# The load of the next batch's z one column later, and the Strassen form for three more tiles, in an attention unit followed by an MoE layer

## The chip, the cores and the metric

The kernel runs on one core of a Trainium2 chip. The metric is the device time of one execution in microseconds (us). In ten executions the kernel before took 1233.96 us in the median (1233.74 to 1235.21).

## The reference

```python
batch, seq, d_model = (8, 3008, 256); d_qk = 64
scores = scale * np.matmul(z, z.transpose(0, 2, 1))     # scale = 1 / seq
attn = np.maximum(scores, 0.0) ** 2
x = (u * np.matmul(attn, v)).reshape(batch * seq, d_model)
h = x @ w_in                                            # d_ff = 2048
g = h * np.cos(h)
out = (g @ w_out).astype(np.float32)
```

All inputs and the output are float32; the kernel computes on float16 tiles and sums in float32.

## The kernel before, in words

**Tiles and stages.** The 3008 rows of a batch are six columns J of 512 (the last one 448). Eight batches make NSLOT = 48 stages s = 6 b + J. A stage has two phases on TensorE. In *phase A* (`phase_a`) the attention output of column s is summed over all rows (L258), into the two PSUM banks M for the first half of d and a pair of banks E for the second. Between these matmuls stand the score matmuls (L191) of later columns, about 3 stages ahead, each followed by relu on ScalarE (L204) and square on VectorE (L209, L212). The scores are symmetric, so half of them are not computed but transposed by a DMA that SP (SyncE) issues (L238, L244). At its end `gate_sum` (L269, L270) and `gate_mul` (L286) make x = u * attention; the second half of the product is made by GpSimd (POOL) at the beginning of phase B.

In *phase B* (`phase_b`) the MoE layer runs on 512 rows, called tile m. It holds h of tile s-1 and y of tile s-2. h comes in eight *units* of two 128-wide blocks of d_ff: four matmuls into one tile E (L403), cos by ScalarE into c (L411), and g = h * cos on VectorE (L414). There are three tiles E, so a unit's matmuls wait for the g of the third unit before. The units come in the order 0, 4, 1, 5, 2, 6, 3, 7. Tile g has two buffers (`gpool`): g of tile m takes the buffer of tile m-2. Tile x has two buffers as well.

**The Strassen form.** For tiles that `mixed` names (2 to 45, without those of 384 rows: 5, 17, 29, 41) y is not four plain products over 256 rows, but the seven of a Strassen scheme (the Winograd variant), each 16 matmuls of 128 x 128 (L465): 112 matmuls of 128 columns instead of 64 of 256. They need sums of blocks of g: `mix_early` on GpSimd makes s1 and a difference in place (L427, L428) once g is there, four pairs a tile; `mix_late` on VectorE makes s2 and s4 (L433, L435) during phase A of the next stage. The products run in the order 5, 1, 6, 7, 2, 3, 4 (`order_y`), one after each h unit, in turns into the banks M[0] and M[1]; the results are scaled and added by ScalarE (L484), VectorE (L478) and GpSimd (L487, L490), and SP stores them (L529). The other tiles are plain: `emit_y` has two blocks of d_ff for all rows (L507), `store_y` copies (L537) and stores. The last tile has a function of its own, `last_y`, which computes y row block by row block and stores each at once.

**The order.** The order of each engine's instructions is the order of the calls, written by hand (`manual_schedule`); waits between engines follow from the tiles that they share. All loads of u, v and z are issued by GpSimd and convert to float16 (L118, L124, L140, L146), each tile as a whole in its turn of GpSimd's queue. All DMA transpositions are issued by SP.

**z.** The z of batch b+1 goes through one buffer (`zpool`) in two halves. `load_z` loads a half twice, side by side (L118; the second half has four small issues L124 as well), `turn_z` transposes it by DMA into zT (L133). In the main loop, for b > 0: `load_z(b+1, 0)` behind phase A of J=0; `turn_z(b+1, 0)` and straight behind it `load_z(b+1, 1)` behind phase A of J=1; `turn_z(b+1, 1)` behind phase A of J=2. The second load overwrites the buffer that the first transposition reads. For b = 0 the same pair stands behind phase B of stage 2.

**The start.** Stages 0 to 2 have phases A of their own (`phase_a_first`). Four units of tile 0 stand between those of stages 1 and 2; phase B of stage 2 has units 4 to 7 of tile 0 and 0 to 5 of tile 1, that of stage 3 the last two of tile 1 and then all of tile 2. The end: phase B of stage 46 has h of tile 45 and y of 44, stage 47 h of 46 and y of 45, stage 48 (no phase A) h of 47 and y of 46; then `last_y(47)`.

Of the kernel before, what the change touches and what calls it, by code (L numbers as in the profile page):

```python
# [10 lines left out]
FP32 = mybir.dt.float32  # L11
# [3 lines left out]
def kernel(  # L15
# [9 lines left out]
    nc = tc.nc  # L25
# [77 lines left out]
    def take_e():  # L103
        i = e_order.pop(0)
        e_order.append(i)
        return i
# [119 lines left out]
    def emit_turns(due, more=0):  # L226
        while turns and (turns[0][0] <= due or more > 0):
            if turns[0][0] > due:
                more -= 1
            (b, c), key = turns.pop(0)  # L230
            b, J, I = key
            i = turn_slots[key]
            a = piece_bufs[i]
            if I == J:
                a4 = a.rearrange("p (k w) -> p k w", w=CW)
                for rr in range(2, 4):
                    rows = P if J * 4 + rr < NB - 1 else H
                    nc.sync.dma_start_transpose(  # L238
                        a4[:, 0:2, rr * P:rr * P + rows],
                        a[0:rows, rr * CW:rr * CW + 2 * P],  # L240
                    )
            else:
                d = new_piece((b, I, J))
                nc.sync.dma_start_transpose(d.rearrange("p (n j) -> p n j", j=P), a)  # L244
            if pending.pop(i) == "dropped":
                free_pieces.append(i)
# [146 lines left out]
    def mwidth(m):  # L393
        return 3 * P if m % (2 * NC) == NC - 1 else CW
# [21 lines left out]
        )  # L416

    def mixed(m):
        return 2 <= m < NSLOT - 2 and mwidth(m) == CW

    F = NFT // 2
    T = 2 * P
# [1 line left out]
    def mix_early(m, j):  # L424
        g, f = gs[m], slice(2 * j, 2 * j + 2)
        lower = slice(F + 2 * j, F + 2 * j + 2)
        nc.gpsimd.tensor_tensor(s1[:, f, :], g[:, f, T:], g[:, lower, T:], ALU.add)  # L427
        nc.gpsimd.tensor_tensor(g[:, f, T:], g[:, f, 0:T], g[:, f, T:], ALU.subtract)  # L428
# [18 lines left out]

    order_y = (5, 1, 6, 7, 2, 3, 4)

    def product(m, n):  # L450
        g = gs[m]
        t = lambda i: w_mix[:, i, :, :]
        left, right = {
            1: (g[:, 0:F, 0:T], w_out16[:, 0:F, 0:P]),
            2: (g[:, F:, 0:T], w_out16[:, F:, 0:P]),
            3: (s4, w_out16[:, F:, P:D]),
            4: (g[:, F:, T:], t(3)),
            5: (s1, t(0)),
            6: (s2, t(1)),
            7: (g[:, 0:F, T:], t(2)),  # L460
        }[n]
        acc = M[order_y.index(n) % 2][:, 0:T]
        for ft in range(F):
            for k in range(2):
                nc.tensor.matmul(  # L465
                    acc[:, k * P:(k + 1) * P],
                    left[:, ft, k * P:(k + 1) * P],
                    right[:, ft, :],
                    start=(ft == 0 and k == 0),
                    stop=(ft == F - 1 and k == 1),  # L470
                )
        acc = acc.rearrange("p (k d) -> p k d", d=P)
        if n == 5:
            y_outs[m] = [opool.tile([P, 2, D], FP32, name="o") for i in range(2)]
            y_parts[m] = {}
        c11, c12, c21, c22 = (y_outs[m][i][:, :, d * P:(d + 1) * P] for i in range(2) for d in range(2))
        parts = y_parts[m]
        add = lambda dst, other: nc.vector.scalar_tensor_tensor(  # L478
            dst, acc, inv_s2, other, ALU.mult, ALU.add
        )  # L480
        if n in (1, 5, 6):
            parts[n] = ypool.tile([P, 2, P], FP32, name=f"p{n}")
        if n in (1, 5):
            nc.scalar.activation(parts[n], acc, AF.Copy, bias=0.0, scale=inv_s2)  # L484
        elif n == 6:
            add(parts[6], parts[1])
            nc.gpsimd.tensor_tensor(c12, parts[6], parts[5], ALU.add)  # L487
        elif n == 7:
            add(c21, parts[6])
            nc.gpsimd.tensor_tensor(c22, c21, parts[5], ALU.add)  # L490
        elif n == 2:
            add(c11, parts[1])
        elif n == 3:
            add(c12, c12)
            store_half(m, 0, y_outs[m][0])
        else:
            add(c21, c21)
            store_half(m, 1, y_outs[m][1])

    def y_bank(m, k):  # L500
        if m == NSLOT - 1 and k == 3:
            return E[0][:, 0, 0:D]
        return M[k // 2][:, (k % 2) * D:(k % 2 + 1) * D]

    def y_block(m, ft, k):
        final = m == NSLOT - 1
        nc.tensor.matmul(  # L507
            y_bank(m, k),
            gs[m][:, ft, k * P:(k + 1) * P],
            w_out16[:, ft, :],  # L510
            start=(ft == 0 and (k % 2 == 0 or (final and k == 3))),
            stop=(ft == NFT - 1 and (k % 2 == 1 or k == mwidth(m) // P - 1 or (final and k == 2))),
        )

    def emit_y(m, i):
# [17 lines left out]
    def store_y(m):  # L533
        for half in range(2):
            n = min(2, mwidth(m) // P - 2 * half)
            o = opool.tile([P, 2, D], FP32, name="o")
            nc.scalar.activation(  # L537
                o[:, 0:n, :],
                M[half].rearrange("p (k d) -> p k d", d=D)[:, 0:n, :],
                AF.Copy, bias=0.0, scale=inv_s2,  # L540
            )
            store_half(m, half, o)

    def last_y(m):
        b, J = m // NC, m % NC
        for ft in range(NFT):
            y_block(m, ft, 0)
            y_block(m, ft, 1)
        for k in range(4):
            if k >= 2:  # L550
                for ft in range(NFT):
                    y_block(m, ft, k)
            o = opool.tile([P, 2, D], FP32, name="o")
            nc.scalar.activation(
                o[:, 0, :], y_bank(m, k),
                AF.Copy, bias=0.0, scale=inv_s2,
            )
            t0 = b * S + J * CW + k * P
            if k < 3:
                nc.sync.dma_start(out[t0:t0 + P, :], o[:, 0, :])  # L560
            else:
                nc.sync.dma_start(out[t0:t0 + H, :], o[0:H, 0, :])
                nc.scalar.dma_start(out[b * S - H:b * S, :], o[H:P, 0, :])

    def phase_b(s):
        y, hs = s - 2, [(s - 1, i) for i in (0, 4, 1, 5, 2, 6, 3, 7)]
        if s == 2:
            hs = [(0, i) for i in range(4, 8)] + [(1, i) for i in range(6)]
        elif s == 3:
            hs = [(1, 6), (1, 7)] + hs  # L570
        elif s == NSLOT + 1:
            hs = []
        for dh in range(len(late_sums)):
            gate_mul(s, 2 - len(late_sums), late_sums.pop(0), nc.gpsimd)
        if mixed(y):
            ys = [lambda n=n: product(y, n) for n in order_y]
        else:
            ys = [lambda i=i: emit_y(y, i) for i in range(8)]
            if len(hs) == 8:
                six, seven = ys[6:]  # L580
                ys[6:] = [lambda: (six(), seven(), store_y(y))]
            else:
                ys[7] = lambda f=ys[7]: (f(), store_y(y))
        n = 0
        for i, (m, unit) in enumerate(hs):
            times_c = emit_h(m, unit)
            if not mixed(y):
                times_c()
            if i < len(ys):
                ys[i]()  # L590
            if mixed(y):
                times_c()
            if mixed(m) and unit >= 4:
                mix_early(m, unit - 4)
            if i in (1, 3, 5):
                emit_turns((0, 0), 1)

    parts0 = [(4 * g, 4 * g + 4) for g in range(NC)]
    nc.vector.memset(warm, 0.0)
# [82 lines left out]
    phase_a_first(0, 12, {4: lambda: turn_late(4), 8: lambda: turn_late(5)})  # L682
    phase_a_first(1, 12)
    nc.gpsimd.dma_start(w_out16, moe_w_out.rearrange("(k p) f -> p k f", p=P))
    for i in range(4):
        emit_h(0, i)()
    phase_a_first(2, 14)
    assert done_groups[0] == need[3]
# [10 lines left out]
    for s in range(3, NSLOT + 1):  # L699
        b, J = s // NC, s % NC  # L700
        if s < NSLOT - 2:
            load_u(s + 2)
        if s < NSLOT:
            phase_a(s)
        if b + 1 < B:
            if b > 0 and J == 0:
                load_z(b + 1, 0)
            if b > 0 and J == 1:
                turn_z(b + 1, 0)
                load_z(b + 1, 1)  # L710
            if J == (2 if b > 0 else 3):
                turn_z(b + 1, 1)
            if J == NC - 2:
                load_v(b + 1, 0)
            if J == NC - 1:
                for g in range(1, NC):
                    load_v(b + 1, g)
        if s < NSLOT - 2:
            turn_u(s + 2)
        phase_b(s)  # L720
# [31 lines left out]
```

## Time and profile before

| | |
|---|---|
| median of ten executions | 1233.96 us |
| the profiled execution | 1235.2 us |
| its span, first to last instruction | 1233.4 us |
| TensorE matmul busy | 1196.5 us (97%) |
| VectorE, ScalarE, GpSimd busy | 990.9, 796.2, 645.6 us |
| phase B of an undisturbed stage with a full tile in Strassen form | 13.27 us |
| mean granted TensorE clock | 0.989 |

In the lines of the profile PE is TensorE (PEld its weight loads), DVE VectorE, ACT ScalarE, POOL GpSimd, SP SyncE, with a q where the queue alone issues. L118 is line 118 of the kernel, `out<-in` the tiles it writes and reads. A line of the view of waits has who waited at which line, for whom, the sum in us, how often, and the longest. A row of the timeline has start and length in us, engine, line, operation and tiles, how many were merged, and in brackets how long the engine had stood idle before it and what ended that. A row of the groups has, behind the count, busy us and the mean of one in ns, then the idle time before.

### The profile page before, as it was taken

Reading aid. Unit: us, or ns where it says so; the run is one execution under the profiler, and the core shown is the slowest. Engines: PE = TensorE matmul, PEld = TensorE weight load, DVE = VectorE, ACT = ScalarE, POOL = GpSimd, SP = SyncE. Lnnn points to the kernel's source line nnn. Section 1 sums busy time; section 2 is a strip of 40 time slices with the busy share of each in tenths; the row PEclk is TensorE's granted clock in tenths of the full one; section 3 lists DMA queues with packets and bytes.
Section 4 is the critical chain, followed back from the end, with each engine's and each line's share of the span. In section 5 each row is a group of like instructions: output and inputs, shape, how many; then the busy total and the mean of one; then the engine's idle time right before and its main releaser. Section 6 shows DMA issues by size and latency. Waiting matters only on the chain.

```text
span 1233.4 us, 28309 instructions
## 1 busy us (share of the span) xinstructions
PE 1196.5 (97%) x11695; PEld 708.1 (57%) x11695; DVE 990.9 (80%) x1248; ACT 796.2 (65%) x923; POOL 645.6 (52%) x657
## 2 busy tenths in 40 slices
PE   8999999999979999999998999999999799999998
PEld 4455655655546655665564655665566465566566
DVE  6857887889868887788986889778888588978765
ACT  7857676667646666667674667666766467666444
POOL 3155725657455671665645657176563665525540
PEclk9999999999989999999998999999999899999999
DMA  9998897769966599755996469973797635974301
GB/s 154 167 168 142 134 139 101 116 116 134 138 97 107 100 137 152 116 94 107 150 154 100 73 116 143 165 105 77 114 172 123 107 69 107 152 140 87 60 18 53
DMA packets 467410, 145.13 MB, mean 118 GB/s; under 512 B 391760, under 2 KB 467024, under 8 KB 467280
## 3 DMA queue, kind: packets, MB, share of 16 engines
q1 hardware_dynamic: 368304, 110.11, 51.1%
q0 software_dynamic: 97440, 32.78, 26.1%
q8 instruction: 91, 1.49, 0.5%
q10 hardware_dynamic: 1536, 0.43, 0.2%
q14 instruction: 39, 0.32, 0.1%
HBM read 66.32 MB, written 24.64 MB: 74 GB/s over the span
## 4 chain that ended last, share of the span: by engine, by line
PE 86%; POOL 5%; DVE 3%; DMA 2%; issue 2%; ACT 2%; SPq 0%; POOLq 0%; DVEq 0%; ACTq 0%
PE E L403 24%; PE M L465 19%; PE M L258 18%; PE E L258 17%; PE E L191 5%; PE M L507 3%; DMA zT<-z 2%; ACT r L204 1%; POOL s L427 1%; POOL g L428 1%; POOL z L124 1%; POOL z L118 1%; DVE A L209 1%; POOL x L286 1%; DVE sm L270 1%
## 5 line engine op out<-in xcount | busy, mean ns | idle before, releaser
L411 ACT ACTIVATE c<-E 128x1024 f16<-128x1024 f32 (+1 forms) x384 | 386.0, 1007 | 230.8 <-PE E L403 229.9
L414 DVE SCALAR_TENSOR_TENSOR g<-E,c 128x1024 f16<-128x1024 f32 (+1 forms) x384 | 458.4, 1197 | 74.7 <-ACT c L411 74.2
L204 ACT ACTIVATE r<-E 128x512 f16<-128x512 f32 (+1 forms) x342 | 327.9, 967 | 142.1 <-PE E L191 137.2
L258 PEld LDWEIGHTS <-v 64*128 64x128 f16 x4512 | 228.8, 95 | 275.5 <-issue 45.2
L403 PE MATMUL E<-x,w_in 128*128 128x512 f16 (+1 forms) x1408 | 355.2, 375 | 7.6 <-DVE sm L270 6.8
L258 PE MATMUL M<-A,v 64*128 64x512 f16 (+1 forms) x2256 | 288.9, 378 | 21.7 <-DVE o L478 21.4
L258 PE MATMUL E<-A,v 64*128 64x512 f16 (+1 forms) x2256 | 278.1, 372 | 0.0
L427 POOL TENSOR_TENSOR s<-g 128x512 f16<-128x512 f16 x160 | 188.5, 1178 | 141.3 <-DVE g L414 104.6
L428 POOL TENSOR_TENSOR g<-g 128x512 f16<-128x512 f16 x160 | 200.8, 1255 | 12.5
L403 PEld LDWEIGHTS <-w_in 128*128 128x128 f16 x1536 | 135.0, 98 | 118.0 <-issue 28.4
L209 DVE TENSOR_TENSOR A<-r 128x1024 f16<-128x1024 f16 x240 | 175.5, 742 | 22.7 <-ACT r L204 22.1
L465 PEld LDWEIGHTS <-g 128*128 128x128 f16 x2560 | 156.4, 98 | 36.0
L286 POOL TENSOR_TENSOR x<-sm,uT 128x512 f16<-128x512 f32 (+1 forms) x43 | 49.0, 1139 | 192.6 <-DVE sm L270 192.3
L465 PEld LDWEIGHTS <-s 128*128 128x128 f16 x1920 | 117.3, 98 | 27.0
L191 PE MATMUL E<-zT 64*128 64x512 f16 (+2 forms) x684 | 126.8, 363 | 2.2 <-DVE zT L631 1.1
L433 DVE TENSOR_TENSOR s<-s,g 128x1024 f16<-128x1024 f16 x80 | 88.0, 1101 | 13.9 <-POOL s L427 13.9
L118 POOL DMA_DIRECT2D z<-in_z_dram x28 | 29.9, 1071 | 130.5 <-DMA zT<-z 130.5
L212 DVE TENSOR_TENSOR A<-r 128x512 f16<-128x512 f16 (+1 forms) x102 | 79.1, 776 | 19.1 <-ACT r L204 18.9
L465 PE MATMUL M<-w_mix,g 128*128 128x128 f16 x1280 | 84.5, 219 | 0.0
L465 PE MATMUL M<-w_mix,s 128*128 128x128 f16 x1280 | 84.5, 219 | 0.0
L465 PE MATMUL M<-w_out,g 128*128 128x128 f16 x1280 | 84.5, 219 | 0.0
L478 DVE SCALAR_TENSOR_TENSOR o<-M,o 128x256 f32<-128x256 f32 x80 | 34.0, 424 | 41.8 <-POOL o L487 24.0
(55 smaller groups left out, 715.7 us busy)
## 6 DMA issues: line engine op xcount, KB each, us to landing
out_dram<-o SPq DMA_DIRECT2D x87, 256.0 KB, 2.2
v<-in_v_dram POOLq DMA_DIRECT2D x40, 256.0 KB, 8.9
u<-in_u_dram POOLq DMA_DIRECT2D x40, 256.0 KB, 5.0
A<-A SPq DMA_TRANSPOSE x207, 5.1
z<-in_z_dram POOLq DMA_DIRECT2D x14, 192.0 KB, 10.9
z<-in_z_dram POOLq DMA_DIRECT2D x14, 176.0 KB, 4.1
v<-in_v_dram POOLq DMA_DIRECT2D x8, 192.0 KB, 11.9
u<-in_u_dram POOLq DMA_DIRECT2D x8, 192.0 KB, 4.1
```

Source lines behind the costliest of these rows:

```text
L191: nc.tensor.matmul(e[:, t, 0:W], zT[t * H:(t + 1) * H, k * P:(k + 1) * P], zT[t * H:(t + 1) * H, J * CW:J * CW + W], start=True, stop=True,)
L204: nc.scalar.activation(r[:, :, 0:W], e[:, :, 0:W], AF.Relu)
L209: nc.vector.tensor_tensor(a4, r4, r4, ALU.mult)
L212: nc.vector.tensor_tensor(a4, r[:, :, 0:W], r[:, :, 0:W], ALU.mult)
L258: nc.tensor.matmul(bank[:, 0:width(J)], vs[b, k // 4][t * H:(t + 1) * H, k % 4, dh * P:(dh + 1) * P], value_rhs(b, J, k, t), start=start, ...
L403: nc.tensor.matmul(e[:, f, 0:W], w_in16[:, k, ft * P:(ft + 1) * P], x[:, k, 0:W], start=(k == 0), stop=(k == 1),)
L411: nc.scalar.activation(c[:, :, 0:W], e[:, :, 0:W], AF.Sin, bias=half_pi, scale=inv_s2)
L414: return lambda: nc.vector.scalar_tensor_tensor(gs[m][:, 2 * i:2 * i + 2, 0:W], e[:, :, 0:W], 1.0, c[:, :, 0:W], ALU.mult, ALU.mult)
L427: nc.gpsimd.tensor_tensor(s1[:, f, :], g[:, f, T:], g[:, lower, T:], ALU.add)
L428: nc.gpsimd.tensor_tensor(g[:, f, T:], g[:, f, 0:T], g[:, f, T:], ALU.subtract)
L433: nc.vector.tensor_tensor(s2[:, f, :], s1[:, f, :], g[:, f, 0:T], ALU.subtract)
L465: nc.tensor.matmul(acc[:, k * P:(k + 1) * P], left[:, ft, k * P:(k + 1) * P], right[:, ft, :], start=(ft == 0 and k == 0), stop=(ft == F - ...
```

## The change

Three things change.

1. `load_z(b+1, 1)` stands at the beginning of stage J=2 (for b > 0), behind the load of u and ahead of phase A, and no longer directly behind `turn_z(b+1, 0)` in J=1. For b = 0 nothing moves.
2. `mixed` names tiles 1, 46 and 47 too. Two units of tile 0, not four, stand ahead of phase A of stage 2; phase B of stage 2 has 14 units, the last six of tile 0 and all eight of tile 1, and y of tile 0 between them; stage 3 has the eight of tile 2 and the seven products of tile 1.
3. At the end, phase B of stage 46 has four units (0, 4, 1, 5) of tile 46 behind the eight of tile 45; stage 47 the other four of 46 and four of 47; stage 48 the last four of 47. What is summed early for tile 46 is still on GpSimd, in stage 47; for tile 47 it is on VectorE (`last_early`). The late sums of 46 and 47 (`mix_late`) stand between the g of these phases. `last_y` has seven products in the order 1, 2, 4, 5, 7, 6, 3, in the banks M and in two tiles E of two banks each.

`multiply`, `add_to` and `copy_to` are `product` cut into parts, for `last_y`.

```diff
     def mixed(m):
-        return 2 <= m < NSLOT - 2 and mwidth(m) == CW
+        return 1 <= m and mwidth(m) == CW
...
+    def last_early(m, c):
+        g, f = gs[m], slice(4 * c, 4 * c + 4)
+        lower = slice(F + 4 * c, F + 4 * c + 4)
+        nc.vector.tensor_tensor(s1[:, f, :], g[:, f, T:], g[:, lower, T:], ALU.add)
+        nc.vector.tensor_tensor(g[:, f, T:], g[:, f, 0:T], g[:, f, T:], ALU.subtract)
+
     def last_y(m):
         b, J = m // NC, m % NC
-        for ft in range(NFT):
-            y_block(m, ft, 0)
-            y_block(m, ft, 1)
-        for k in range(4):
...
+        t0 = b * S + J * CW
+        ea, eb = E[take_e()], E[take_e()]
+        banks = {1: M[1], 2: M[0], 4: ea[:, 0, :], 5: ea[:, 1, :], 7: eb[:, 0, :], 6: eb[:, 1, :], 3: M[1]}
+        o = [opool.tile([P, 2, D], FP32, name="o") for i in range(2)]
...
+        for n in (1, 2, 4, 5, 7, 6, 3):
+            multiply(m, n, banks[n][:, 0:T])
+            acc = banks[n][:, 0:T].rearrange("p (k d) -> p k d", d=P)
+            if n == 1:
+                copy_to(p[1], acc)
+            elif n == 2:
+                add_to(c11, acc, p[1])
+                nc.sync.dma_start(
+                    out[t0:t0 + T, 0:P].rearrange("(k p) d -> p k d", p=P), c11
+                )
+            elif n == 4:
+                copy_to(c21, acc)
+            elif n == 5:
+                copy_to(p[5], acc)
+                nc.gpsimd.tensor_tensor(c12, p[1], p[5], ALU.add)
+            elif n == 7:
+                add_to(c22, acc, p[1])
+            elif n == 6:
+                add_to(c12, acc, c12)
+                add_to(p[6], acc, c22)
+                nc.vector.tensor_tensor(c22, p[6], p[5], ALU.add)
+                nc.vector.tensor_tensor(c21, p[6], c21, ALU.add)
+                store_half(m, 1, o[1])
             else:
...
+                for k, eng in enumerate((nc.sync, nc.scalar)):
+                    add_to(c12[:, k, :], acc[:, k, :], c12[:, k, :])
+                    eng.dma_start(out[t0 + k * P:t0 + (k + 1) * P, P:D], c12[:, k, :])
 
     def phase_b(s):
         y, hs = s - 2, [(s - 1, i) for i in (0, 4, 1, 5, 2, 6, 3, 7)]
         if s == 2:
-            hs = [(0, i) for i in range(4, 8)] + [(1, i) for i in range(6)]
-        elif s == 3:
-            hs = [(1, 6), (1, 7)] + hs
-        elif s == NSLOT + 1:
-            hs = []
+            hs = [(0, i) for i in range(2, 8)] + hs
+        elif s == NSLOT - 2:
+            hs = hs + [(s, i) for i in (0, 4, 1, 5)]
+        elif s == NSLOT - 1:
+            hs = hs[4:] + [(s, i) for i in (0, 4, 1, 5)]
+        elif s == NSLOT:
+            hs = hs[4:]
...
+        tail = {}
+        if s == NSLOT - 1:
+            tail = {
+                1: [lambda: [mix_early(s - 1, j) for j in range(3)]],
+                3: [lambda: mix_early(s - 1, 3)],
+                4: [lambda: mix_late(s - 1, "s2", 0)],
+                5: [lambda: mix_late(s - 1, "s2", 1)],
+                6: [lambda: mix_late(s - 1, "s4", 0)],
+                7: [lambda: mix_late(s - 1, "s4", 1)],
+            }
+        if s == NSLOT:
+            after = (0, 1, 2)
+        elif s == NSLOT - 2:
+            after = (0, 2, 3, 5, 7, 8, 10)
+        elif n > 8:
+            after = (1, 2, 4, 5, 7, 8, 10, 11)
+        elif mixed(y):
+            after = range(7)
+        else:
+            after = (0, 1, 2, 3, 4, 5, 6, 6)
...
-            if i < len(ys):
-                ys[i]()
+            for f, place in zip(ys, after):
+                if place == i:
+                    f()
             if mixed(y):
                 times_c()
-            if mixed(m) and unit >= 4:
+            if mixed(m) and unit >= 4 and m < NSLOT - 2:
                 mix_early(m, unit - 4)
+            for f in tail.get(i, ()):
+                f()
+            if s == NSLOT and i in (1, 3):
+                last_early(s - 1, i // 2)
             if i in (1, 3, 5):
                 emit_turns((0, 0), 1)
+        if s == NSLOT:
+            ys[3]()
+            ys[4]()
+            mix_late(s - 1, "s2", 0)
+            ys[5]()
+            mix_late(s - 1, "s2", 1)
+            ys[6]()
+            mix_late(s - 1, "s4", 0)
+            mix_late(s - 1, "s4", 1)
...
-    for i in range(4):
+    for i in range(2):
         emit_h(0, i)()
     phase_a_first(2, 14)
...
         if s < NSLOT - 2:
             load_u(s + 2)
+        if b > 0 and J == 2 and b + 1 < B:
+            load_z(b + 1, 1)
         if s < NSLOT:
             phase_a(s)
...
             if b > 0 and J == 1:
                 turn_z(b + 1, 0)
-                load_z(b + 1, 1)
```

In `phase_b`, `after` says behind which unit each part of y stands; `ys` are these parts.

## The prediction

> **What bounds the kernel now.** I read the page's shares first, then who waited for whom, then the timeline at the waits.
>
> ```profile
> span 1233.4 us, 28309 instructions
> PE 1196.5 (97%) x11695; PEld 708.1 (57%) x11695; DVE 990.9 (80%) x1248; ACT 796.2 (65%) x923; POOL 645.6 (52%) x657
> ```
>
> TensorE is the bound: 36.9 us of the span are not its own. Who owns them, from the view of waits (total, times, longest):
>
> ```profile
> POOL z L118 <- DMA zT<-z: 130.5, 7, 23.3
> ...
> DVE o L478 <- POOL o L487: 24.0, 3, 8.6
> ...
> PE M L258 <- DVE o L478: 21.4, 3, 7.7
> ...
> PE E L403 <- DVE sm L270: 6.8, 4, 2.0
> ```
>
> The first line is GpSimd standing at the load of the second half of the next z. The next two are three times each, so one chain. The timeline of stage 13 (b=2, J=1) shows it:
>
> ```profile
> 336.17 1.04 PE L403 MATMUL E<-x,w_in 128*128 128x512 f16 x4
> ...
> 341.37 1.57 SPq L133 DMA_TRANSPOSE zT<-z  x1
> ...
> 346.66 1.08 POOL L118 DMA_DIRECT2D z<-in_z_dram  x1 [16.29 <-DMA zT<-z]
> ...
> 351.00 1.21 POOL L286 TENSOR_TENSOR x<-sm,uT 128x512 f16<-128x512 f32 x1
> ...
> 354.50 0.72 POOL L487 TENSOR_TENSOR o<-p,p 128x256 f32<-128x256 f32 x1
> ...
> 355.25 0.42 DVE L478 SCALAR_TENSOR_TENSOR o<-M,o 128x256 f32<-128x256 f32 x1 [8.53 <-POOL o L487]
> ...
> 357.19 2.74 PE L258 MATMUL M<-A,v 64*128 64x512 f16 x12 [7.69 <-DVE o L478]
> ```
>
> GpSimd is held at L118 until the transposition lands, pays 4.3 us for six load issues, then starts its gate and mixing 14.83 us into phase B. VectorE waits for the sum L487, and bank M stays full when phase A of stage 14 wants it. The clock then suffers too (window, busy times, then the granted clock):
>
> ```profile
> 965.00:970.00 5.00, 4.79 (x24) 1.99 (x25) 3.59 (x5) 0.60 (x1) 4.76 (x6) 0.50 0.27 80
> ```
>
> At the start another wait stands, in stage 3:
>
> ```profile
> 86.20 0.69 DVE L286 TENSOR_TENSOR x<-sm,uT 128x512 f16<-128x512 f32 x1 [6.83 <-PE E L403]
> 86.46 1.15 POOL L118 DMA_DIRECT2D z<-in_z_dram  x1 [14.21 <-DMA zT<-z]
> ...
> 89.02 1.02 PE L403 MATMUL E<-x,w_in 128*128 128x512 f16 x4 [1.98 <-DVE sm L270]
> ```
>
> The gate of tile 3 overwrites the x buffer that h of tile 1 still reads, and that h stands in the next phase B.
>
> [...]after 7.7 us idle the clock was 0.50 over five us. [...]L286 had its data and stood behind L118. [...]L433 beside GpSimd's mixing means 1101 ns, its like L435 683.
>
> **The change, part by part.** Lengths are differences of timeline starts: phase B from its first L403 to the first L258 behind it, phase A the reverse.
>
> *z load.* Six of the seven waits are moved (b=1 to 6; that of b=0 stays). What they cost TensorE: for b=2, 4, 6 phase B of J=1 takes 21.02, 19.34, 21.06 against 13.27 undisturbed, 21.6 together, and phase A behind it 12.77, 13.23, 14.24 against 11.42, 6.0 (the clock). For b=1, 3, 5, whose y has no sum on GpSimd, phase B of J=2 takes 15.22, 14.90, 15.02 against 13.27 at the same place of b=7: 5.3. Sum 32.9. What the moved issues cost: two L118 at 1.07 and four L124 at 0.57 are 4.4 us of GpSimd. At b=7, where no z is loaded, GpSimd ends its stage at 1119.6 and next works at 1126.58, so 1119.6 + 4.4 = 1124.0 fits. The last large piece, issued at 1121.9, lands 4.1 later by the page's row of DMA issues, the small ones 3.1 after theirs, so all by 1127; SP is past its own transpositions (the last L244 at 1125.20, 2.14 long) at 1127.3, so it finds the second half there; behind that stand the u of two stages on and the y stores. I cost it at nothing; if the landing slips, SP slips with it. Gain 32.9, at least 26.3 (the PE gaps alone: 7.69+6.01+7.73+1.80+1.47+1.60).
>
> *Start.* Before phase A of stage 2 two h units stand, not four: scores wait for the first g, not the third, and begin 2.3 earlier (42.82 to 40.5); the phase runs on ScalarE back to back, so it ends at 53.5 instead of 55.81. A unit with its product takes 1.757 (six pairs from 1197.13 to 1207.67 in stage 47), 0.87 and 0.885, a plain y part 0.87 (1209.40 to 1210.27). Phase B of stage 2 has 14 units and 8 parts, 22 x 0.87 = 19.1, with 0.3 of gaps to 72.9 (72.09 before). Phase A of stage 3, 11.4: 84.3; the 6.83 wait is gone. Phase B of stage 3 is then 8 units and 7 products, 13.27, not 19.55. But GpSimd's z wait of b=0 stays, now under a y with sums: L286 started at 92.68, 8.4 into that phase. Starts 14.83, 13.18 and 14.89 into it gave stalls of 7.69, 6.01, 7.73, start minus 7.15, so 1.2 here. End 98.8 against 102.94: gain 4.1, the saving of tile 1's products included (0.77: 8 x 0.87 - 7 x 0.885).
>
> *Tail.* h of tile 46 goes half into stage 46, h of 47 half into 47; both become mixed. In the built program the first g of tile 46 waits for the last matmul of product 4 of tile 44, whose g buffer it takes; likewise 47 after 45. VectorE, in order, stands there. Stage 46: product 4 ends at 11 x 0.87 + 7 x 0.885 = 15.7; g then takes 1.2 before the twelfth unit has its bank (17.2), and the add that frees M comes after two g: 18.75 instead of 13.27. Loss 5.5, 3.5 of it the four units. From stage 47's phase B (0 here, 1195.37 before) two groups by form and three rows of the timeline give the pace:
>
> ```profile
> L414 DVE SCALAR_TENSOR_TENSOR g<-E,c 128x1024 f16<-128x1024 f32 x352 | 427.9, 1219 | 70.9 <-ACT c L411 70.9
> L435 DVE TENSOR_TENSOR s<-g,s 128x1024 f16<-128x1024 f16 x80 | 54.5, 684 | 0.0
> ```
>
> ```profile
> 1206.78 1.06 PE L465 MATMUL M<-w_mix,g 128*128 128x128 f16 x16
> 1207.67 1.03 PE L403 MATMUL E<-x,w_in 128*128 128x512 f16 x4
> 1207.94 0.43 DVE L478 SCALAR_TENSOR_TENSOR o<-M,o 128x256 f32<-128x256 f32 x1 [0.20 <-PE M L465]
> ```
>
> That last add reads product 4: at 12.57 VectorE may start on tile 47. Before product 3 of tile 46 gets bank M1 it owes eight g (1.19 in a row), four adds (0.40) and eight 1024-wide f16 sums (0.66; four are the new first sums of tile 47, moved here from GpSimd): 16.4, so 28.9. GpSimd's mixing of tile 46 (four pairs of 1.16 and 1.25) ends at 14.2 and is not what is late, ScalarE's moved c (1.02 each) run under g. On the way TensorE stands at each bank E that waits for a g (units eight to twelve), which this sum holds already, since product 3 waits longest. Then nine products, 8.0: 36.9. Product 5 of tile 47 shares a tile with product 4, whose copy waits for a store of tile 46 (2.2 to landing): 0.9; product 6 waits for the add of 7: 0.5. TensorE ends at 38.3. Behind product 6 stand four VectorE operations of 0.42[...], then the last adds; SP has three stores of 0.45 to issue before its last: 40.6; from there 3.3 as now (last copy done 1230.05, end 1233.4). End 43.9 against 38.03: loss 5.9. TensorE would need 29.0 for the same work, so VectorE is the bound here. Its 3.2 us idle before product 3 may lower the clock, as 1.98 did at 89.02; unknown, 0 to 3 by the L258 case, I take 0.6. The f16 sums may take 1.1 beside GpSimd: +1 at most, and an overlap I missed gives as much back. Tail: loss 12.0, bounds 0 (all hidden) to 17.
>
> Sum: -32.9 - 4.1 + 12.0 = -25.0. The profiled execution took 1235.2 with a span of 1233.4; its span becomes 1208.4. The median of the runs is 1233.96, so 1209.0.
>
> **Rivals.** *Tail hidden.* If VectorE's work at the end overlaps as TensorE's saving would have it, the tail costs nothing: 1233.96 - 37.0 = 1197. For: VectorE is only 80% busy overall. Against: the new work falls in one stretch of 30 us, each piece in front of a bank that TensorE needs. *The wait comes back.* The second half lands late, SP holds there, and transpositions or stores behind it cost half the gain: 1209 + 16 = 1225; or GpSimd still stands at L118, one column later. For: issue to landing of z was 3.6 to 15.1. Against: the transposition that the load waits for landed at 194.59 in stage 7, and GpSimd comes to the new place only behind that stage's mixing, six us after phase B's end (1119.6 against 1113.54 at b=7), so near 205. *Slower.* The same transposition on SP holds the y stores and the A transpositions so long that phase A of J=3 stalls in all six batches. To lose 0.2% each must cost (25.0+2.5)/6 = 4.6 us; with 15.1 to landing SP would be 11 late, while its next A transposition stood 12.9 behind it (218.93, 231.79), so it decides only from a landing of some 21 us: then above 1236. None in the trace is so late.
>
> **How the numbers follow.** Forecast 0.78, its own range 1201 to 1217; tail hidden 0.10; wait back 0.09; slower 0.02; something that undoes it all 0.01. Range 1200 to 1219, which leaves out most of the rivals and little of the forecast. The measurement tells 0.2%, 2.5 us, from no change: faster 0.96, same 0.01, slower 0.03.
>
> **What would show it.** Right: GpSimd's wait at the z load falls from 130.5 in 7 to some 14 in 1; TensorE's wait at L258 for VectorE almost gone; every phase B of J=1 and 2 near 13.27; stage 3's near 14.5; the view of waits has about 12 us of TensorE waiting for VectorE behind stage 46, most at bank M before product 3 and at E for h. Wrong: a TensorE gap in the last 40 us under 4 us in sum (tail too dear), SP waiting for z in front of L133 with A late behind it (z gain too large), or phase B of stage 3 above 16.

## The result, and the profile after

The kernel after takes 1210.01 us in the median of eight runs (1208.93 to 1212.15) against 1234.18 for the kernel before (29 runs on the same chips): 0.9805 of its time, 95% interval 0.9797 to 0.9814, so 24.2 us less. 1209.0 was forecast. The profiled execution has a span of 1208.2 us against 1233.4; the sum in the prediction gave 1208.4.

The page of the kernel after begins:

```profile
span 1208.2 us, 28680 instructions
PE 1188.9 (98%) x11839; PEld 705.7 (58%) x11839; DVE 1008.3 (83%) x1282; ACT 794.7 (66%) x922; POOL 664.4 (55%) x678
```

36.9 us of the span were not TensorE's own before, 19.3 are now. The view of waits of after, with the waiter, its line, whom it waited for, the sum, how often, the longest:

```profile
SPq L133 <- DMA z<-in_z_dram: 1.6, 4, 0.6
...
POOL z L118 <- DMA zT<-z: 4.2, 1, 4.2
...
PE E L403 <- DVE g L414: 3.8, 3, 1.4
PE M L464 <- DVE o L473: 3.0, 1, 3.0
...
PE E L464 <- ACT o L476: 1.7, 1, 1.7
...
PE M L258 <- DVE o L473: 0.4, 1, 0.4
```

GpSimd stood 130.5 us in seven waits for the transposition of z; 4.2 us in one are left. TensorE's 21.4 us of waiting at L258 for VectorE have become 0.4. What TensorE waits for now is new and lies at the end (L403, L464). SP, which the prediction let find the second half of z landed, stands there for 1.6 us in all.

Stage 13 in the timeline of after (start, length, engine, line, operation, in brackets the idle time and what ended it), from the beginning of phase B of J=1 into phase A of J=2:

```profile
328.88 1.04 PE L403 MATMUL E<-x,w_in 128*128 128x512 f16 x4
330.45 1.15 POOL L286 TENSOR_TENSOR x<-sm,uT 128x512 f16<-128x512 f32 x1 [7.37 <-DVE sm L270]
333.56 1.81 SPq L133 DMA_TRANSPOSE zT<-z  x1
336.42 0.73 POOL L494 TENSOR_TENSOR o<-p,p 128x256 f32<-128x256 f32 x1
342.15 1.04 PE L258 MATMUL M<-A,v 64*128 64x512 f16 x8
348.20 1.09 POOL L118 DMA_DIRECT2D z<-in_z_dram  x1
358.16 1.41 SPq L133 DMA_TRANSPOSE zT<-z  x1
```

GpSimd's gate L286 begins 1.57 us into the phase and not 14.83, its sum L494 begins 7.5 us into it (L487, the same sum before: 354.50 - 336.17 = 18.3), and the phase takes 342.15 - 328.88 = 13.27. The transposition still goes out 4.7 us into the phase and lands 5.2 later; nobody waits for it, since the load that overwrites its buffer comes at 348.20.

The start, from phase B of stage 3:

```profile
84.35 1.04 PE L403 MATMUL E<-x,w_in 128*128 128x512 f16 x4
84.77 1.15 POOL L118 DMA_DIRECT2D z<-in_z_dram  x1 [4.24 <-DMA zT<-z]
...
90.99 1.21 POOL L286 TENSOR_TENSOR x<-sm,uT 128x512 f16<-128x512 f32 x1
...
97.61 1.47 PE L258 MATMUL M<-A,v 64*128 64x512 f16 x12
```

The phase takes 13.26. The end has VectorE waiting for a g buffer, and TensorE for VectorE and ScalarE:

```profile
1175.25 1.22 DVE L414 SCALAR_TENSOR_TENSOR g<-E,c 128x1024 f16<-128x1024 f32 x1 [3.19 <-PE M L464]
1176.53 1.02 PE L403 MATMUL E<-xodd,w_in 128*128 128x512 f16 x4 [1.41 <-DVE g L414]
...
1190.96 1.86 PE L464 MATMUL M<-w_out,s 128*128 128x128 f16 x16 [3.00 <-DVE o L473]
...
1198.57 1.05 PE L464 MATMUL E<-w_mix,s 128*128 128x128 f16 x16 [1.70 <-ACT o L476]
```

Stretches of 5 us of after (bounds, length, busy times and counts of PE, PEld, DVE, ACT, POOL, then the granted clock, DMA share and GB/s):

```profile
1180.00:1185.00 5.00, 4.92 (x55) 3.41 (x53) 5.00 (x6) 3.37 (x5) 0.00 (x0) 1.00 0.17 56
1185.00:1190.00 5.00, 2.14 (x33) 1.87 (x32) 4.90 (x8) 1.02 (x1) 0.72 (x1) 1.00 0.00 0
1190.00:1195.00 5.00, 4.04 (x50) 4.04 (x50) 3.99 (x8) 0.00 (x0) 0.73 (x1) 0.66 0.14 48
```

VectorE is full for ten microseconds, TensorE is busy 2.14 of the second five, and then the clock falls to 0.66: product 3 takes 1.86 us and the one behind it 1.56, instead of 1.06.

By phases, before against after in the two profiled executions: the twelve stages J=1 and J=2 of b = 1 to 6 gained 32.9; from the first instruction to the end of phase B of stage 3 gained 102.94 - 97.61 = 5.3; stage 46's phase B lost 18.77 - 13.27 = 5.5, and from stage 47's phase B (1162.64) to the end 45.55 - 38.03 = 7.5. Sum -32.9 - 5.3 + 13.0 = -25.2, the difference of the spans.

### The profile page after: what moved, and what is told of

The parts are those of the page before. It is cut to its first block, busy times and chain, and to the rows that moved or that the text cites. A ratio compares the mean times of both kernels' runs of the same rounds, so it can differ in the third digit from the quotient of the medians.

```text
span 1208.2 us, 28680 instructions
## 1 busy us (share of the span) xinstructions
PE 1188.9 (98%) x11839; PEld 705.7 (58%) x11839; DVE 1008.3 (83%) x1282; ACT 794.7 (66%) x922; POOL 664.4 (55%) x678
## 4 chain that ended last, share of the span: by engine, by line
PE 95%; DVE 2%; ACT 1%; issue 1%; DMA 1%; DVEq 0%; ACTq 0%
PE E L403 27%; PE M L464 21%; PE M L258 20%; PE E L258 19%; PE E L191 6%; PE M L511 2%; DVE g L414 1%; ACT r L204 1%; DMA out_dram<-o 0%; DMA z<-in_z_dram 0%; DVE o L473 0%; PE E L464 0%; DVE sm L270 0%; DVE s L551 0%; DVE s L433 0%
## 5 line engine op out<-in xcount | busy, mean ns | idle before, releaser
L258 PEld LDWEIGHTS <-v 64*128 64x128 f16 x4512 | 226.1, 94 | 252.3 <-issue 19.2
L403 PE MATMUL E<-x,w_in 128*128 128x512 f16 (+1 forms) x1408 | 353.3, 375 | 1.4 <-DVE g L414 1.4
L427 POOL TENSOR_TENSOR s<-g 128x512 f16<-128x512 f16 x168 | 196.9, 1172 | 168.6 <-DVE g L414 130.4
L258 PE MATMUL M<-A,v 64*128 64x512 f16 (+1 forms) x2256 | 283.3, 372 | 0.8 <-DVE o L473 0.4
L258 PE MATMUL E<-A,v 64*128 64x512 f16 (+1 forms) x2256 | 278.0, 372 | 0.0
L428 POOL TENSOR_TENSOR g<-g 128x512 f16<-128x512 f16 x168 | 207.5, 1235 | 13.2
L403 PEld LDWEIGHTS <-w_in 128*128 128x128 f16 x1536 | 134.4, 98 | 114.6 <-issue 24.1
L464 PEld LDWEIGHTS <-g 128*128 128x128 f16 x2752 | 168.3, 98 | 38.4 <-issue 0.9
L286 POOL TENSOR_TENSOR x<-sm,uT 128x512 f16<-128x512 f32 (+1 forms) x43 | 48.6, 1132 | 244.4 <-DVE sm L270 244.1
L464 PEld LDWEIGHTS <-s 128*128 128x128 f16 x2064 | 126.7, 98 | 33.9 <-issue 5.8
L433 DVE TENSOR_TENSOR s<-s,g 128x1024 f16<-128x1024 f16 x86 | 96.3, 1121 | 1.0 <-POOL s L427 1.0
L464 PE MATMUL M<-w_out,g 128*128 128x128 f16 x1376 | 90.7, 219 | 0.8 <-DVE p L473 0.8
L464 PE MATMUL M<-w_mix,g 128*128 128x128 f16 x1344 | 89.2, 220 | 0.0
L464 PE MATMUL M<-w_mix,s 128*128 128x128 f16 x1344 | 88.7, 219 | 0.0
L191 PEld LDWEIGHTS <-zT 64*128 64x128 f16 x684 | 35.6, 94 | 42.0 <-issue 4.4
L435 DVE TENSOR_TENSOR s<-g,s 128x1024 f16<-128x1024 f16 x86 | 58.6, 684 | 0.0
```

What stands on the lines that cost most here:

```text
L191: nc.tensor.matmul(e[:, t, 0:W], zT[t * H:(t + 1) * H, k * P:(k + 1) * P], zT[t * H:(t + 1) * H, J * CW:J * CW + W], start=True, stop=True,)
L258: nc.tensor.matmul(bank[:, 0:width(J)], vs[b, k // 4][t * H:(t + 1) * H, k % 4, dh * P:(dh + 1) * P], value_rhs(b, J, k, t), start=start, ...
L403: nc.tensor.matmul(e[:, f, 0:W], w_in16[:, k, ft * P:(ft + 1) * P], x[:, k, 0:W], start=(k == 0), stop=(k == 1),)
L433: nc.vector.tensor_tensor(s2[:, f, :], s1[:, f, :], g[:, f, 0:T], ALU.subtract)
L464: nc.tensor.matmul(acc[:, k * P:(k + 1) * P], left[:, ft, k * P:(k + 1) * P], right[:, ft, :], start=(ft == 0 and k == 0), stop=(ft == F - ...
```

## Experiments

Ten kernels, each executed four or five times, beside the kernel before on the same chip (its median 1234.23, 1235.27 and 1234.63 in the three groups: runs one to four, five to eight, nine and ten). The kernel before differs by 1.0 us between these groups, so a difference of about that size against another group's median says little alone; for such a difference the lengths of the phases decide. The diffs show the lines that matter, with `...` where lines are left out.

**1. The z load alone**, on the kernel before.

```diff
+        if b > 0 and J == 2 and b + 1 < B:
+            load_z(b + 1, 1)
         if s < NSLOT:
             phase_a(s)
...
                 turn_z(b + 1, 0)
-                load_z(b + 1, 1)
```

> The kernel before, with nothing changed but the place of the second half of the next z (start of J=2 for b > 0). My theory: six of GpSimd's seven waits go, worth 32.9 us as worked out from the phases; about 1201 us, and phase B of J=1 and J=2 of every batch near 13.27 us. First rival (the wait comes back, the moved load lands late): half of it, about 1217, with SP waiting for z ahead of L133. Second rival (the z load was worth only its bare TensorE gaps, and the rest of the gain in the whole change is the start's): 26.3, about 1208.

1201.04 us, ratio 0.9730 (0.9717 to 0.9743): 33.2 us less. Every phase B of J=2, and of J=1 at even b, takes 13.27 (at odd b J=1 takes 12.25, as before; from stage 47's to the end it is 38.05, as before). Both rivals fall: half of the gain, and the bare gaps of 26.3; the slower phase A behind a stall belongs to what the wait cost. One part of the change alone is faster than all of it.

**2. Without the new end**: the kernel after, with tiles 46 and 47 plain and `phase_b` and `last_y` of before at the end.

```diff
-        return 1 <= m and mwidth(m) == CW
+        return 1 <= m < NSLOT - 2 and mwidth(m) == CW
...
-        elif s == NSLOT - 2:
-            hs = hs + [(s, i) for i in (0, 4, 1, 5)]
-        elif s == NSLOT - 1:
-            hs = hs[4:] + [(s, i) for i in (0, 4, 1, 5)]
-        elif s == NSLOT:
-            hs = hs[4:]
```

> The changed kernel with the last two tiles plain and the end as in the kernel before: the z load and the start remain. My theory: the new tail loses 13.0 us in the trace of after (5.5 in stage 46, 7.5 behind it), so about 1197 us, faster than both kernels; from phase B of stage 47 to the end 38.0 again. Rival (the tail costs nothing and something else in after loses, or the start and the tail are tied to each other): 1208 to 1210.

1198.09 us, ratio 0.9706 (0.9693 to 0.9719): 11.9 faster than the whole change, where 13.0 was expected. 0.8 of the missing 1.1 is at the end: from stage 47's phase B on it takes 38.80, not 38.0 (see run 10). The rest is at the start, where phase A of stage 4 begins 0.33 later than in after.

**3. The new end alone**, on the kernel before (`last_y`, the lists of units and the late sums as in the change).

```diff
-        return 2 <= m < NSLOT - 2 and mwidth(m) == CW
+        return 2 <= m and mwidth(m) == CW
...
+        elif s == NSLOT - 2:
+            hs = hs + [(s, i) for i in (0, 4, 1, 5)]
```

> The kernel before, with the Strassen form and the new order for tiles 46 and 47 alone. My theory: 13.0 us slower, about 1247 us, stage 46's phase B 18.8 and stage 47's to the end 45.5. Rival (VectorE's work at the end is hidden, and the loss in after comes from the stages ahead being faster): not slower than 1236.

1246.70 us, ratio 1.0102 (1.0088 to 1.0115): 12.5 us slower. Phase B of stage 46 takes 18.77, and from stage 47's to the end 44.65, with the same waits as in after (2.99 before product 3 of tile 46, clock 0.70 behind it). The loss is the end's own and doesn't come from faster stages ahead of it.

**4. The new start alone**, on the kernel before.

```diff
-            hs = [(0, i) for i in range(4, 8)] + [(1, i) for i in range(6)]
-        elif s == 3:
-            hs = [(1, 6), (1, 7)] + hs
+            hs = [(0, i) for i in range(2, 8)] + hs
...
-    for i in range(4):
+    for i in range(2):
         emit_h(0, i)()
```

> The kernel before, with the new start alone: tile 1 in Strassen form, two units of tile 0 ahead of stage 2, the rest in stage 2. My theory: 5.3 us by the phases of after, about 1229 us; phase B of stage 3 is 13.3 and has no stall, since GpSimd's gate begins less than 7.15 us into it. Rival (as the prediction had it, a stall of 1.2 us before phase A of stage 4): 4.1, about 1230, phase B of stage 3 near 14.5. Rival (the start only moves work from one stage to the other): within 1 us of 1234.

1230.27 us, ratio 0.9964 (0.9951 to 0.9976): 4.0 us less by the medians, 4.4 by the ratio. Phase B of stage 3 takes 13.27 without a stall, so the phase account of the first expectation holds; the interval (3.0 to 6.0 us) holds 5.3 and 4.1 alike, so it is the trace that decides. The 5.3 also contains a fall of the clock: phase B of stage 3 takes 19.55 us in the profiled execution of before, and 17.87 in run 5, which has the same wait there and no fall (granted clock 0.57 and 1.00 from 90 to 94 us; last section). Without that fall the same phases would give some 3.7 (an estimate: 5.3 less 19.55 - 17.87); the medians lie between. Part of the start's gain is given back at the other end, where 38.67 us stand against 38.05.

The three parts alone make -33.2 - 4.0 + 12.5 = -24.7; together they made -24.2. Within the noise they add up: none of them needs another.

**5. The load left, what it waits for moved**, on the kernel before.

```diff
+        if 0 < b < B - 1 and J == 1:
+            turn_z(b + 1, 0)
         if s < NSLOT:
             phase_a(s)
...
-                turn_z(b + 1, 0)
                 load_z(b + 1, 1)
```

> The kernel before with the load of the second half of z left where it stood, but the transposition of the first half, which that load waits for, called ahead of phase A of J=1 and not behind it. My theory: what cost the time was GpSimd standing at L118, so the gain of the moved load (33 us) comes in this way too: GpSimd is free some 16 us before 346.66 in stage 13, pays its 4.3 us of load issues before phase B begins, and its gate is in time; 1201 to 1203 us. Rival (what helped was that the six load issues left the stretch ahead of phase B, or that VectorE and ScalarE met something else there): 1215 us or more.

1200.82 us, ratio 0.9722 (0.9709 to 0.9735), as much as the moved load gave. So it was GpSimd's standing at L118, not the place of the six issues. But this run has 46.2 us of that wait left, in four pieces (at b = 0, 1, 3 and 5). The waits' view of this run, and stage 7 in its timeline:

```profile
POOL z L118 <- DMA zT<-z: 46.2, 4, 13.8
```

```profile
181.48 1.08 POOL L118 DMA_DIRECT2D z<-in_z_dram  x1 [11.09 <-DMA zT<-z]
...
187.00 1.15 POOL L286 TENSOR_TENSOR x<-sm,uT 128x512 f16<-128x512 f32 x1 [1.15 <-DVE sm L270]
```

11.09 us of waiting cost nothing: they end early enough that the six issues are paid before the gate is wanted, and the gate waits for VectorE's sum. It begins 1.56 us into the phase (185.44), as it does in stage 13 of after (1.57), where no load stands ahead of it.

**6. The old place for odd b only**, on the kernel after.

```diff
-        if b > 0 and J == 2 and b + 1 < B:
+        if b > 0 and b % 2 == 0 and J == 2 and b + 1 < B:
             load_z(b + 1, 1)
...
                 turn_z(b + 1, 0)
+                if b % 2:
+                    load_z(b + 1, 1)
```

> The changed kernel with the second half of z loaded at the old place again for b = 1, 3, 5, and at the new one for b = 2, 4, 6. My theory: at odd b the tile whose y stands in phase B of J=1 has 384 rows and is plain, needs no sum of GpSimd, and the wait costs only what phase B of J=2 lost, 5.3 us for the three: 1215 us, GpSimd waiting about 16 us three times. Rival (every wait of GpSimd costs TensorE the same, a sixth of 32.9 each): 16.4 us, 1226.

1215.24 us, 5.2 above the kernel after. The median is as expected, but not all of it is the waits: phase B of J=2 takes 14.85, 14.70 and 14.68 at b = 1, 3, 5, so the waits cost 4.4 us together, where before had 5.3; the other 0.9 of the profiled execution lies ahead of phase A of stage 4 (98.53 for 97.61), where the edit changes nothing. The length of the waits was expected wrongly: 22.8, 22.6 and 22.6 us, not 16. The longest waits are the cheapest: three of 23 us cost 4.4 together here and 5.3 in before, while in the kernel before three of 14.6 to 16.3 us, at even b, cost 27.6. Timeline of this run, from phase B of stage 7 into that of stage 8, which begins at 206.26:

```profile
190.28 1.08 POOL L118 DMA_DIRECT2D z<-in_z_dram  x1 [22.80 <-DMA zT<-z]
...
194.61 1.22 POOL L286 TENSOR_TENSOR x<-sm,uT 128x512 f16<-128x512 f32 x1
...
205.46 0.69 DVE L433 TENSOR_TENSOR s<-s,g 128x1024 f16<-128x1024 f16 x1 [2.16 <-POOL s L427]
...
210.65 0.68 DVE L270 TENSOR_TENSOR sm<-E,sm 128x512 f32<-128x512 f32 x1
...
211.37 0.81 PE L403 MATMUL E<-x,w_in 128*128 128x512 f16 x3 [1.43 <-DVE sm L270]
```

The y in phase B of stage 7 has no sum on GpSimd, so nobody there waits for it. Its early sums are carried into phase A of the next stage, where VectorE waits for them at L433 (2.16 us), adds L270 late, and bank E comes free 1.43 us late for h: another and much cheaper way from the same wait to TensorE.

**7. Without the early sums of tile 47**, on the kernel after. It leaves these sums out (L551 and L552; the expectation names them one line too far on).

```diff
-            if s == NSLOT and i in (1, 3):
-                last_early(s - 1, i // 2)
```

> The changed kernel without the four early sums of tile 47 on VectorE (L552, L553); it leaves that work out, so tile 47's y is formed of other sums. My theory: VectorE's queue sets when product 3 of tile 46 gets its bank, so the four sums of 0.66 us come off in full: product 3 at 25.7 us after phase B of stage 47 began and not at 28.3, TensorE's wait there 0.4 us or less and not 3.0; 1207.4 us, and up to 2 less if the clock then stays up. Rival (product 3 waits for ScalarE's c or for the bank alone): 1210 us, and the wait stays near 3.

1207.01 us (ratio to before 0.9775, 0.9761 to 0.9788), 3.0 less than after. PE rows of this run's timeline, at product 3 of tile 46 and at product 5 of tile 47:

```profile
1188.87 1.05 PE L464 MATMUL M<-w_out,s 128*128 128x128 f16 x16 [0.92 <-DVE o L473]
...
1195.76 1.87 PE L464 MATMUL E<-w_mix,s 128*128 128x128 f16 x16 [2.26 <-ACT o L476]
```

Product 3 begins 26.6 us after the phase (1162.28) and not 28.3: 1.7 less, where 2.65 was expected, and it still waits 0.92. The larger part of the sums' time comes off, so VectorE's queue sets this point. Not all of it comes off: without the sums VectorE itself stands 0.73 us, for TensorE (0.44) and for ScalarE (0.29). The profiled execution was the slowest of the four (1208.74, mean clock 0.997): in it the clock fell twice, to 0.79 over 1180 to 1185 and, behind the wait for ScalarE's copy, to 0.66 over 1195 to 1200. The three others had 1.000 and took 1206.63 to 1207.34.

**8. The products of stage 46 first**, on the kernel after.

```diff
         elif s == NSLOT - 2:
-            after = (0, 2, 3, 5, 7, 8, 10)
+            after = range(7)
```

> The changed kernel with the seven products of tile 44 behind the first seven units of stage 46, one each, so that product 4 is done before the first unit of tile 46 needs its g buffer. My theory: the g of tile 46 no longer waits for product 4 of tile 44; phase B of stage 46 takes about 16.8 us (12 units of 0.87 and 7 products of 0.885) and not 18.77, and the gap of 1.4 us there goes: 1208.1 us. Rival (VectorE's pace of 1.2 us a g sets that phase, and the wait only moves): 1210 us, phase B of stage 46 above 18.

1209.00 us. That is 1.0 less than after by the medians and 1.9 by the ratios to before (0.9790 and 0.9805), so the phases must tell: phase B of stage 46 takes 17.79 and not 18.77, 1.0 less, half of what was expected. The timeline, at the units of tile 46:

```profile
1147.69 2.90 PE L403 MATMUL E<-x,w_in 128*128 128x512 f16 x12
1151.09 2.15 PE L403 MATMUL E<-x,w_in 128*128 128x512 f16 x8 [0.50 <-DVE g L414]
```

The wait for the g buffer was worth some 1.0 us; behind it VectorE's 1.2 us for a g (1219 ns in the mean in after), against TensorE's 0.87 for a unit, still holds these five units, which stand in a row (0.50 here, and some 0.3 inside the row: eight matmuls take 2.15 us, and 1.89 at 1148.02 in after). Both theories had a part of it.

**9. Filler ahead of product 3**, on the kernel after.

```diff
             mix_late(s - 1, "s2", 0)
+            for i in range(13):
+                nc.tensor.matmul(E[e_order[0]][:, 0, :], w_in16[:, 0, 0:P], w_in16[:, 0, 0:CW], start=True, stop=True)
             ys[5]()
```

> The changed kernel with 13 matmuls of 512 columns more ahead of product 3 of tile 46, into a bank E that is overwritten later; TensorE runs them in the 3 us in which it stood idle there (13 x 0.216 = 2.8). My theory: the idle time itself stays lost, but the granted clock no longer falls behind it (0.66 over 1190 to 1195 in the trace of after, 5 x 0.34 = 1.7 us): 1208.3 us. Rival (the clock falls for what went before, the gaps at 1176 to 1179, or the lower clock costs nothing because VectorE sets the pace): 1210 us or, with the matmuls late, up to 1211.

1207.54 us (ratio to before 0.9782, 0.9769 to 0.9796), 2.5 less than after, from work that computes nothing. PE rows of the timeline, then stretches of 5 us:

```profile
1187.70 2.97 PE L650 MATMUL E<-w_in 128*128 128x512 f16 x13
1190.65 1.05 PE L464 MATMUL M<-w_out,s 128*128 128x128 f16 x16
...
1196.12 1.05 PE L464 MATMUL E<-w_mix,s 128*128 128x128 f16 x16 [0.84 <-ACT o L476]
```

```profile
1175.00:1180.00 5.00, 2.89 (x11) 1.16 (x11) 5.00 (x7) 1.02 (x1) 0.52 (x1) 0.82 0.18 57
1180.00:1185.00 5.00, 5.00 (x56) 4.05 (x55) 4.95 (x7) 3.35 (x5) 0.00 (x0) 0.84 0.15 51
...
1190.00:1195.00 5.00, 5.00 (x83) 4.55 (x80) 4.41 (x9) 0.39 (x1) 0.72 (x1) 1.00 0.31 103
```

Product 3 begins at 28.5 us, no sooner than in after, but takes 1.05 and not 1.86, and the products behind it run at full clock. From product 3's start to the end of product 4 of tile 47 it is 1195.28 - 1190.65 = 4.63 us, and 1196.87 - 1190.96 = 5.91 in after. So the fall of the clock cost 1.3 us there. That is less than the 1.7 expected, because the clock stood at 0.50 for 3.4 us (in after 0.50 from 1190.5 to 1193.5, 0.76 and 0.83 in the half microseconds beside them) and some 0.7 of these fell into the stall itself, which ended at 1190.96. Of the two profiled executions' 2.0 us between phase B of stage 47 and the end (43.56 for 45.55), 0.9 more is the shorter wait for ScalarE's copy, less 0.15 of a later product 3.

That the filler kept the clock up is not shown by this trace. In it the clock fell ten microseconds earlier (0.82 and 0.84 in the stretches), behind TensorE's gaps of 1.41 and 1.04 us that end at 1176.07 and 1178.13, as the rival had it, and VectorE sets the pace there. Run 8 has no filler, and its profiled execution shows the same: the clock falls early, and then stays up behind a wait of 2.78 us.

```profile
1190.63 1.05 PE L464 MATMUL M<-w_out,s 128*128 128x128 f16 x16 [2.78 <-DVE o L473]
```

```profile
1180.00:1185.00 5.00, 5.00 (x53) 3.80 (x52) 4.95 (x7) 3.06 (x5) 0.00 (x0) 0.81 0.17 54
...
1190.00:1195.00 5.00, 4.37 (x79) 4.37 (x79) 4.40 (x9) 0.39 (x1) 0.73 (x1) 1.00 0.32 102
```

From product 3's start to the end of product 4 of tile 47 run 8 takes 4.63 us too. What speaks for the filler is all executions taken together: the five with it have mean clocks of 0.998 and 0.999 and take at most 1208.46 us, those of run 8 have 0.996 to 0.998, those of after 0.996 to 0.999, and the fastest of the eight of after takes 1208.93. Some of the 2.5 us is not the clock, as the wait for ScalarE's copy shows.

**10. Copies of their own**: run 2, with the last two copies of the last tile in ypool's tiles.

```diff
+            if k < 2:
+                o = opool.tile([P, 2, D], FP32, name="o")
+            else:
+                o = ypool.tile([P, 2, P], FP32, name=f"p{(1, 5)[k - 2]}")
+                o = o.rearrange("p a b -> p (a b)").unsqueeze(1)
-            o = opool.tile([P, 2, D], FP32, name="o")
             nc.scalar.activation(
```

> The changed kernel with the plain end (as the run without the new tail), and the last two copies of the last tile in tiles of their own (the partial sums of ypool, free by then) and not in the two o buffers that stores still read. My theory: in that run ScalarE's third copy waited for a store, and its last copy came 0.84 us after TensorE's last matmul: 1197.2 us against 1198.1. Rival (SP, whose three stores took 4.3 us to issue, sets the end instead): 1198 us.

1197.17 us, ratio 0.9695 (0.9682 to 0.9709): 0.9 less than run 2 and the fastest kernel here, 37.5 us below the kernel before. ScalarE's rows at the end, of run 2 and then of this run:

```profile
1192.21 0.38 ACT L561 ACTIVATE o<-M 128x256 f32<-128x256 f32 x1 [3.28 <-DMA out_dram<-o]
1192.52 0.38 ACT L561 ACTIVATE o<-E 128x256 f32<-128x256 f32 x1
```

```profile
1189.87 0.38 ACT L565 ACTIVATE p<-M 128x256 f32<-128x256 f32 x1 [1.04 <-PE M L514]
1191.62 0.38 ACT L565 ACTIVATE p<-E 128x256 f32<-128x256 f32 x1 [1.36 <-PE E L514]
```

The third copy waited for a store to give back its buffer (3.28 in run 2, 3.15 in run 4, 1.6 in the kernel before), and in runs 2 and 4 that reached the last one. Why the store gives it back later there, with the same end as in the kernel before, is open. SP's stores follow the copies and don't set the end. Stage 47's phase B to the end takes 38.00 again.

## Why the prediction was right, and where it was not

**The z load** held in size and in mechanism: 32.9 forecast, 32.9 by the phases, 33.2 alone. The chain GpSimd at L118, late gate and sum, VectorE at L478, bank M, phase A is supported from two sides: take the load away (run 1) or take its wait away (run 5), and the same time comes back. The split into three dear waits at even b and three cheap ones at odd b held (run 6: 4.4 us for the three cheap ones, 5.3 forecast). The moved issues cost nothing, as forecast, but with less to spare than the 0.3 us it had worked out at b=7: SP stands at L133 in four places, 0.6 at most, and the A transpositions behind it were not late, since no phase changed by it.

**The start** was mis-sized by 1.2 us. Scores, phase A of stage 2, phase B of stage 2 (ends at 73.04, forecast 72.9) and phase A of stage 3 (84.35, forecast 84.3) came as worked out. The step that failed is "L286 started at 92.68, 8.4 into that phase ... so 1.2 here". It took the moment of GpSimd's gate from the one profiled execution of before. In after the gate starts at 90.99, 6.64 into the phase, too early to cost anything, because SP's transposition of the first half of z, behind the y stores of tile 0, goes out 2.6 us earlier and lands 1.7 earlier. SP's row in before, then in after:

```profile
81.41 2.61 SPq L133 DMA_TRANSPOSE zT<-z  x1
```

```profile
78.84 2.21 SPq L133 DMA_TRANSPOSE zT<-z  x1
```

That this comes from the new start is not shown. In runs 1 and 3, which have the start of before, the transposition goes out at 78.63 and 78.23 too, and in run 6, which has the new start, at 80.61: the moment moves by some 3 us from one execution to another, and why is open. So phase B of stage 3 at 13.3, and not near 14.5, was in part luck. The rule behind the 1.2, start minus 7.15, held: in the eight profiled executions with the new start the gate begins 6.12 to 7.35 us into the phase, and only the two latest have a longer phase, 13.34 at 7.11 (run 10) and 13.57 at 7.35 (run 6); there it is start minus some 7.05. (Two of the starts that the rule came from are 13.15 and 14.86 in the trace, not 13.18 and 14.89; that changes nothing.) The sign given for GpSimd, a wait of "some 14", failed for another reason: the four pairs of early sums of tile 1 now lie ahead of the load in its queue, and 4.2 us of idleness are left.

**The end** cost 13.0 by the phases and 12.5 alone, 12.0 was forecast. Stage 46 is as worked out, 18.77 for 18.75, with its 1.38 and 0.44 us of TensorE gaps; what of it is the g buffer is some 1.0 (run 8), the rest the four units and VectorE's pace. Behind it VectorE's sum for product 3 gave 28.9 and it began at 28.3; the wait there is 3.00, forecast 3.2. Two terms were too small. The clock was put at 0.6 where the bounds were 0 to 3, and cost 1.3 (after against runs 8 and 9). The wait for ScalarE's copy was put at 0.9 and was 1.70; it hangs on when a store of tile 46 lands (the copy itself stood 2.6 us for that store in after), and was 0.59 to 2.26 us in runs 3, 7, 8 and 9. The four VectorE operations behind product 6, two of them f32 sums, were put at 0.42 by the author's estimate and took 0.41 to 0.43 in after. With the clock kept up and that wait at 0.84, as in run 9, TensorE is done 38.4 us after the phase's start (forecast 38.3) and the end is at 43.56 (forecast 43.9 ahead of the 0.6).

**The signs.** From phase B of stage 46 on, TensorE's gaps add up to 10.3 us; 8.6 of them wait for VectorE, where about 12 were forecast, and 1.7 for ScalarE. Most are at bank E for h and at bank M before product 3, as said. In the last 40 us they are 8.5, where under 4 would have made the forecast wrong. The rivals: the hidden tail is refuted by run 3, the wait that comes back by run 1, and the slower case never came near: SP is 0.6 late where 11 would not have been enough.

The errors, 1.2 too little gained at the start and 1.0 too little lost at the end, nearly cancel. That is luck, and it is why the span was met to 0.2 us. The median is 1.0 above the forecast because the span's difference was carried over to it: the profiled execution of before was 1.2 above its kernel's median, and that of after (1209.96) was at its own.

## What to carry to other kernels

Price a wait by when the waiting engine next owes something, not by its length: here 23 us cost 1.4 to 2.0, some 16 us cost 9, and 11 us cost nothing. Where a change has parts in different stages, sum each stage's own bound: the end was cut for TensorE, while VectorE, buffers and then the clock set the time there, and leaving that part out gives 1198 instead of 1210. When an engine's queue gets new work ahead of a wait, take that work off the wait before carrying the old number over.

## What was not expected of the hardware

**A wait of 1.98 us was followed by a fall of the clock in one run and by none in another.** Run 1 and run 5 have the same TensorE wait, 1.98 us, at the same place of stage 3. Stretches of 4 us behind it, first of run 1 and then of run 5:

```profile
90.00:94.00 4.00, 4.00 (x20) 2.39 (x19) 2.28 (x3) 1.61 (x2) 1.77 (x3) 0.59 1.41 205
```

```profile
90.00:94.00 4.00, 4.00 (x31) 2.77 (x29) 3.49 (x4) 2.31 (x3) 3.71 (x6) 1.00 1.62 162
```

That is phase B of stage 3 in 19.54 and in 17.87 us, 1.67 apart, for one event. The end shows the same: behind TensorE's gaps of 1.41 and 1.04 us at the units of tile 47 the clock fell in runs 7, 8 and 9 (0.79, 0.81 and 0.84 over 1180 to 1185), and not in after (1.00 from 1175 to 1190). In after, behind the wait of 3.00 us, the clock stood at 0.50 from 1190.5 to 1193.5, with 0.76 and 0.83 in the half microseconds beside them, as much as 3.4 us at 0.50; here 0.59 over 4 us is as much as 3.3 (4 x 0.41 / 0.5). In run 1 a single wait of 1.98 us was enough, with TensorE busy for all the rest of 86 to 94 us, and in run 7 the clock fell to 0.66 over 1195 to 1200 behind one of 2.26. Why a fall follows the same wait in one run and not in the next is not shown.

**The clock was worth most where TensorE was the bound.** In runs 8 and 9 the fall (0.81 and 0.84 over 1180 to 1185), in a stretch paced by VectorE, left product 3 at 28.5 us, 0.15 later than in after, which has no fall there; in after, behind the stall, it cost 1.3 us.
